# Weight sums of a second mixture by accumulating DMAs of GpSimd's queue, and four products of its layer one kept in one PSUM bank

## The chip, the cores and the metric

One core of a Trainium2 chip runs the whole program. The metric is the device time of one execution in microseconds. The engines are named as in the profile: PE is TensorE (PEld its weight load), ACT is ScalarE, DVE is VectorE, POOL is GpSimd, SP is SyncE. A queue that only issues DMAs carries a q (SPq, POOLq).

## The reference, cut to what matters

The program computes an attention with hashed buckets, a first mixture of experts (one expert per token) and a second mixture. The change touches the second mixture alone:

```
def _moe2_ref(x, w_gate, w1, w2):            # x (768, 512), w1 (8, 512, 1024), w2 (8, 1024, 512)
    ...                                      # P (768, 8): the gate, normalised 8 times by rows and columns
    for e in range(8):
        h = np.maximum(x @ w1[e], 0.0)       # layer one
        ye = h @ w2[e]                       # layer two
        out += P[:, e:e + 1] * ye
    return out
```

## The kernel before, in words

Before the second mixture come attention and the first mixture (to about 264 us of the span); both stay as they are.

Second mixture. Numbers are kept as pairs of halves (a high and a low part in float16), so that one product in full precision is three matmuls per 128 rows of the contraction. Expert 0 runs plainly (`plain`, then `gemm2(0)`), the experts 1 to 7 each run `gemm1(e)` and `gemm2(e)`.

`gemm1(e)` computes x times w1[e] with seven products in place of eight. x is cut in four blocks (two halves of the tokens by two halves of the 512 inputs), w1[e] in four quarters A(fh, dh) of 256 inputs (dh) by 512 outputs (fh). The products stand in the order of `PROD`, i = 0 to 6. Each needs one block, or a sum of blocks, of x (made once, `sum_x`), and one quarter, or a sum of quarters, of w1: i = 0, 1 and 6 take the quarters A(0,0), A(0,1) and A(1,1) as they are; i = 2 to 5 take sums of two to four quarters. A product is cut by four chunks j of 128 outputs. For one (i, j), six matmuls of 128x384 go into one PSUM bank; below that is a *group*, and an expert has 28 of them. Behind each group ACT or DVE takes the bank out:

- before, i = 0 is copied to `ta` by ACT (L1688); i = 1 accumulates on top of i = 0 in the same bank, ACT takes its relu (L1690) and the high part of it (L1653), DVE the low part (`low`, L1654);
- i = 2, 3, 4 each have a bank of their own, and DVE adds them to what it holds in SBUF (`add`, L1650); i = 5 and 6 share a bank, DVE adds twice;
- results go through `relu`: the high part by ACT (L1653), the low part by DVE (L1654).

Three matters set the order around this. The weights come by DMA into `raw` tiles (1 MB each, four per expert, an eight-tile ring, issued by SP, L313 and L315). `cut` turns a quarter or a sum into a slot of halves: `hi` by ACT (L1399), then `lo` by DVE (L1402). The sums of quarters are made by DVE just ahead of that (`combo`, L1589, four of 128x1024 per expert). ACT also sums the squares of each raw tile for a scale (`square_w`, L982, two per tile), which PE adds up over the partitions (`norm`, L990). All of these stand as tasks in one list; `work` takes one per group of `gemm1` and one or two per step of `gemm2`, so that most of an expert's cuts and sums run during `gemm2` of the expert before it. Each engine works its own instructions strictly in the order of the program.

`gemm2(e)` computes the second layer into six banks over four rounds r; in the last round DVE scales each bank and adds it to the result (L1774).

Of the kernel before, what the change touches and what calls it, by code (L numbers as in the profile page):

```python
# [8 lines left out]
F32 = mybir.dt.float32  # L9
# [12 lines left out]
P = 128  # L22
# [6 lines left out]
E = 8  # L29
# [193 lines left out]
def kernel(ctx: ExitStack, tc: tile.TileContext, consts, q, k, v, proj, wg, w1, w2, wg2, w12, w22, out, cap, dbg=None):  # L223
# [1154 lines left out]
    def base(e):  # L1378
        return NO0 + NO * (e - 1) if e else 0
# [12 lines left out]
    def cut(n, src=None):  # L1392
        e, i = place_of(n)
        sw = scl[:, 0 if i < 7 else 1, e:e + 1]

        def hi():
            if n not in slot:
                slot[n] = slot_tile(n)
            nc.scalar.activation(out=slot[n][:, 0], in_=src() if src else total[n], func=AF.Copy, scale=sw)  # L1399

        def lo():
            V.scalar_tensor_tensor(  # L1402
                out=slot[n][:, 1], in0=src() if src else total.pop(n), scalar=sw, in1=slot[n][:, 0],
                op0=ALU.mult, op1=ALU.subtract,
            )

        return [hi, lo]
# [81 lines left out]
    def sum_x(o):  # L1489

        for c in range(2):
            in0, in1 = {
                XT1: (ta[:, c], tb[:, c]), XT2: (ta[:, 2 + c], xf(XT1, c)), XT3: (xf(XT2, c), tb[:, c]),
                XT4: (tb[:, 2 + c], xf(XT2, c)),
            }[o]
            V.tensor_tensor(out=xf(o, c), in0=in0, in1=in1, op=ALU.subtract)

    held_x = []
    combine(0)
# [83 lines left out]
    def w1q(e, fh, dh):  # L1583
        return raw_t[4 * NV + 4 * e + fh][:, 2 * dh:2 * dh + 2, :]

    def combo(n, in0, in1, op):
        def go():
            total[n] = sums.tile([P, 2, 512], F32, tag="s", name="s")
            V.tensor_tensor(out=total[n], in0=in0(), in1=in1(), op=op)  # L1589

        return go

    def sums_of(e):
        a = lambda fh, dh: (lambda: w1q(e, fh, dh))
        n = base(e)
        of = lambda m: (lambda: total[n + m])
        return [
            combo(n + 3, a(1, 0), a(1, 1), ALU.add), combo(n + 2, of(3), a(0, 0), ALU.subtract),
            combo(n + 4, a(0, 1), of(2), ALU.subtract), combo(n + 5, a(0, 0), a(1, 0), ALU.subtract),
        ]  # L1600
# [11 lines left out]
    def alloc():  # L1612
        n = state["alloc"]
        if n >= base(E):
            return
        state["alloc"] += 1
        e, i = place_of(n)
        load = [lambda: load_next(nc.scalar if e == 0 else nc.sync)]
        if i > 6:
            r, h = divmod(i - 7, 2)  # L1620
            todo = sq(e + 1, 0, r) if i in (8, 9) else []
            todo = todo + cut(n, lambda: raw_t[4 * NV + 4 * e + 2 + r][:, 2 * h:2 * h + 2, :]) + load * h
        elif e == 0:
            todo = cut(n, lambda: w1q(e, i // 2, i % 2)) + load
            if i == 3:
                todo = todo + sq(e, 1, 0) + sq(e, 1, 1) + [none] * 2 + scale(e, 1)
        elif i < 2:
            todo = ([none] * 2 + scale(e, 0) if i == 0 else []) + cut(n, lambda: w1q(e, 0, i))
            todo = todo + (sums_of(e)[0:2] if i == 0 else sums_of(e)[2:3])
        elif i < 6:  # L1630
            todo = cut(n) + (sums_of(e)[3:4] + load if i == 3 else sq(e, 1, i - 4) if i > 3 else [])
        else:
            todo = cut(n, lambda: w1q(e, 1, 1)) + load + [none] * 2 + scale(e, 1)
        tasks.extend((n, f) for f in todo)
# [11 lines left out]
    blk = lambda b, j, fh, th: hT[:, b, 4 * fh + j, halves[th]]  # L1646
    lows = []

    def add(ps, out, in1):
        V.scalar_tensor_tensor(out=out, in0=ps, scalar=HSH, in1=in1, op0=ALU.mult, op1=ALU.add)  # L1650
# [13 lines left out]
    def gemm1(e):  # L1664
        held, kept = {}, []
        for i, o in enumerate(PROD):
            w = slot[base(e) + i]
            for j in range(4):
                again = i in (1, 6)
                if again:  # L1670
                    ps = held.pop(j)
                    free.append(kept.pop(0))
                elif i in (0, 5):
                    ps = held[j] = bank(kept)
                else:
                    ps = bank()
                n = 0
                ps = ps[:, 0:HW]
                for c in range(2):
                    for a, b in W3:  # L1680
                        nc.tensor.matmul(  # L1681
                            ps, lhsT=w[:, a, c, j * P:(j + 1) * P], rhs=xo[:, o, b, c, :],
                            start=(n == 0 and not again), stop=(n == 5), skip_group_check=again,
                        )
                        n += 1
                u, v, w12_ = ta[:, j], tb[:, j], tcc[:, j % 3]
# [166 lines left out]
```

## Time and profile before

| | us |
|---|---|
| median of 3 runs | 751.83 (750.5 to 755.17) |
| the profiled execution | 750.09 |
| its span | 748.3 |
| second mixture, as part of the span | about 264 to 748 |

The page gives each engine's busy time; the views of stretches and of instructions in order of time give the second mixture, whose seven experts repeat a pattern of some 58.6 us each.

### The profile page before, as it was taken

To read this page: it belongs to the slowest core of one execution; us is meant where nothing else is said; L and a number is where in the kernel's file an instruction comes from. 1 tells how busy PE (TensorE), PEld (TensorE's weight loads), DVE (VectorE), ACT (ScalarE), POOL (GpSimd) and SP (SyncE) were. 2 spreads that over 40 slices of the span, in tenths; PEclk is the share of its full clock that TensorE was granted. 3 is DMA by queue.
4 is the path that set the end of the run, shared out by engine and by line. 5 is a ranking of instruction groups with operands and counts; after the bars stand their busy time and mean duration, and the time that the engine had idled before them with its cause. 6 is when DMAs were issued, how large, how long until landed. Compare 5 with 4: busy or idle time off the path is not lost.

```text
span 748.3 us, 12168 instructions
## 1 busy us (share of the span) xinstructions
PE 725.5 (97%) x4700; PEld 465.2 (62%) x4700; DVE 568.3 (76%) x989; ACT 465.1 (62%) x757; POOL 114.8 (15%) x110
## 2 busy tenths in 40 slices
PE   6899998999999799999999999999999999999998
PEld 6798987877788556545545545545545545645654
DVE  5999998589999866887695785786785865866842
ACT  4698898388788678555653754664575375365420
POOL 5568883612100300000000000000000000000000
PEclk9999998999999999999999999999999999999999
DMA  9546559799998333422131131041033030000002
GB/s 228 128 124 170 157 153 361 276 380 378 385 378 305 88 113 113 168 73 98 63 108 56 38 131 58 3 164 59 1 115 112 1 113 1 1 1 0 1 1 85
DMA packets 61608, 97.02 MB, mean 130 GB/s; under 512 B 17603, under 2 KB 19059, under 8 KB 61546
## 3 DMA queue, kind: packets, MB, share of 16 engines
q1 hardware_dynamic: 53066, 82.21, 33.6%
q10 hardware_dynamic: 7520, 10.83, 4.2%
q0 software_dynamic: 960, 3.15, 1.3%
q8 instruction: 39, 0.64, 0.3%
q14 instruction: 23, 0.19, 0.1%
HBM read 79.99 MB, written 9.31 MB: 119 GB/s over the span
## 4 chain that ended last, share of the span: by engine, by line
PE 62%; DVE 2%; ACT 1%; issue 0%; DVEq 0%
PE b L1756 32%; PE b L1681 25%; PE b L1724 4%; DVE hl L1402 1%; DVE s L1589 1%; PE b L1519 1%; ACT junk L982 0%; DVE q L1253 0%; DVE x L1772 0%; PE b L1478 0%; PE b L990 0%; PE b L1466 0%; ACT hl L1399 0%; PE b L1566 0%; DVE x L1257 0%
## 5 line engine op out<-in xcount | busy, mean ns | idle before, releaser
L1756 PE MATMUL b<-hl,hT 128*128 128x512 f16 (+1 forms) x1176 | 252.0, 375 | 0.0
L1756 PEld LDWEIGHTS <-hT 128*128 128x128 f16 x1176 | 114.3, 98 | 129.1
L1681 PE MATMUL b<-xo,hl 128*128 128x384 f16 x1176 | 192.7, 326 | 0.0
L1681 PEld LDWEIGHTS <-hl 128*128 128x128 f16 x1176 | 114.7, 98 | 77.0 <-issue 0.8
L1402 DVE SCALAR_TENSOR_TENSOR hl<-raw,scl,hl 128x1024 f16<-128x1024 f32 x57 | 72.3, 1281 | 45.0 <-ACT hl L1399 45.0
L338 DVE TENSOR_TENSOR hl<-raw,hl 128x1024 fp32r<-128x1024 f32 x66 | 81.9, 1284 | 4.1 <-ACT hl L336 3.9
L1399 ACT ACTIVATE hl<-raw,scl 128x1024 f16<-128x1024 f32 x57 | 63.1, 1136 | 24.8 <-DVE scl L993 24.8
L336 ACT ACTIVATE hl<-raw 128x1024 fp32r<-128x1024 f32 x72 | 71.8, 1059 | 1.4 <-PE av L770 0.9
L982 ACT ACTIVATE junk<-raw 128x1024 bf16<-128x1024 f32 x64 | 67.1, 1048 | 1.0
L1774 DVE SCALAR_TENSOR_TENSOR x<-b,q,x 128x512 f32<-128x512 f32 (+1 forms) x43 | 31.5, 737 | 34.4 <-PE b L1756 34.0
L1181 PE MATMUL mm<-hl,dT 128*128 128x512 f32 x216 | 54.3, 398 | 1.6 <-DVE dT L1154 1.6
L1654 DVE SCALAR_TENSOR_TENSOR hT<-tz,hT 128x384 f16<-128x384 f32 x44 | 24.1, 555 | 37.6 <-ACT hT L1653 37.4
L761 POOL TENSOR_TENSOR plo<-pf,phi 128x768 f16<-128x768 f32 x30 | 49.3, 1660 | 21.4 <-ACT phi L757 18.7
L1653 ACT ACTIVATE hT<-tc 128x384 f16<-128x384 f32 x28 | 14.6, 523 | 60.2 <-DVE tc L1650 60.2
L1207 PE MATMUL y<-hl,hT 128*128 128x512 f32 x192 | 49.2, 400 | 1.1 <-DVE ysb L1225 1.0
L1399 ACT ACTIVATE hl<-s,scl 128x1024 f16<-128x1024 f32 x28 | 31.4, 1145 | 28.5 <-DVE s L1589 21.5
L750 ACT ACTIVATE pf<-mm 128x384 f32<-128x384 f32 x96 | 42.3, 492 | 10.2 <-PE mm L743 9.2
L696 DVE TENSOR_REDUCE mz<-mm 128x1 f32<-128x384 f32 x96 | 46.9, 547 | 0.9 <-PE mm L689 0.7
L1181 PEld LDWEIGHTS mm<-hl,dT 128*128 128x128 f32 x216 | 39.4, 188 | 10.6 <-DVE dT L1154 2.4
L743 PE MATMUL mm<-q,k 128*128 128x384 f32 x192 | 44.6, 354 | 0.4 <-DVE k L653 0.3
L757 ACT ACTIVATE phi<-pf 128x768 f16<-128x768 f32 x48 | 40.5, 850 | 1.6 <-PE av L770 0.3
L1207 PEld LDWEIGHTS y<-hl,hT 128*128 128x128 f32 x192 | 34.8, 188 | 9.1 <-DVE ysb L1225 1.8
(278 smaller groups left out, 1002.3 us busy)
## 6 DMA issues: line engine op xcount, KB each, us to landing
raw<-in_moe_w_dram SPq DMA_DIRECT2D x48, 1024.0 KB
raw<-in_moe_w_dram SPq DMA_DIRECT2D x48, 256.0 KB
raw<-in_moe_w_dram ACTq DMA_DIRECT2D x8, 1024.0 KB
xd<-zer SPq DMA_DIRECT2D x13, 256.0 KB
xe<-xd SPq DMA_DIRECT2D x7, 256.0 KB
yd<-ysb ACTq DMA_DIRECT2D x7, 256.0 KB
qkin<-in_q_dram SPq DMA_DIRECT2D x8, 192.0 KB
vin<-in_v_dram SPq DMA_DIRECT2D x4, 384.0 KB
```

Of the source, the lines that this page charges most:

```text
L336: nc.scalar.activation(out=t[:, 0], in_=raw[:, sl, :], func=AF.Copy)
L338: lo = lambda eng=eng, sl=sl, t=t: eng.tensor_tensor(out=t[:, 1], in0=raw[:, sl, :], in1=f32(t)[:, 0], op=ALU.subtract)
L696: V.tensor_reduce(out=mz[h][:, a, t:t + 1], in_=b.ps[:, 0:HW], axis=AX.X, op=ALU.max)
L743: nc.tensor.matmul(ps[:, 0:HW], lhsT=kk[h][:, tok(t)], rhs=qq[h][:, half(a)], start=(i == 0), stop=(i == 1))
L761: eng.tensor_tensor(out=lo[h, t], in0=pf[h, t], in1=hi[h, t], op=ALU.subtract)
L982: nc.scalar.activation(out=junk[:, 0:n], in_=src, func=AF.Square, accum_out=acc)
L1181: nc.tensor.matmul(ps, lhsT=dT[e][:, a, c * P:(c + 1) * P], rhs=w(b, c), start=(n == 0), stop=(n == 11))
L1207: nc.tensor.matmul(ps, lhsT=t[:, a, half, f * P:(f + 1) * P], rhs=w(b, f), start=(n == 0), stop=(n == 23))
L1399: nc.scalar.activation(out=slot[n][:, 0], in_=src() if src else total[n], func=AF.Copy, scale=sw)
L1402: V.scalar_tensor_tensor(out=slot[n][:, 1], in0=src() if src else total.pop(n), scalar=sw, in1=slot[n][:, 0], op0=ALU.mult, op1=ALU.subtract,)
L1681: nc.tensor.matmul(ps, lhsT=w[:, a, c, j * P:(j + 1) * P], rhs=xo[:, o, b, c, :], start=(n == 0 and not again), stop=(n == 5), skip_group_ ...
L1756: nc.tensor.matmul(ps, lhsT=hT[:, a, 2 * r + f, t * P:(t + 1) * P], rhs=w[:, b, f, cs], start=(r == 0 and n == 0), stop=(r == 3 and n == 5),)
```

## The change

1. **Sums of quarters.** `combo` and DVE's four additions per expert go. `combine_w` makes them out of DMAs: SP loads one quarter (512 KB) into a tile of `sums`, and GpSimd's queue adds the other quarters to it by DMAs with `accum_op=add`. The sum of i = 2 takes two such additions, i = 4 three, i = 5 one; the sum of i = 3 is made in place, by one addition of A(1,1) onto A(1,0) in the `raw` tile, after ACT has squared it. They are issued one expert ahead: those of i = 2, 4 and 5 right behind the cut that frees the tile of `sums`, that of i = 3 behind the squares. For expert 1 the first six stand at the start of the second mixture.
2. **Signs.** All sums are now additions, so the second half of the outputs is computed with the opposite sign; `sum_x` and the joins of `gemm1` turn it back.
3. **One bank for four products.** i = 0, 2, 3 and 4 now accumulate in one bank per j. ACT copies what stands in it after i = 0 (`ta`), i = 2 (`tb`) and i = 3 (`tz`), and takes the relu after i = 4. i = 1 has a bank of its own, which DVE joins to `ta` (`join`); i = 5 and 6 share a bank, joined to `tz` and `tb`. Per expert DVE has 12 joins where it had 20 additions; ACT has 16 copies out of PSUM where it had 8.
4. **Loads.** The load of the next expert's first raw tile moves from slot 3 to slot 1 of the task list.

```
-    def combo(n, in0, in1, op):
-            total[n] = sums.tile([P, 2, 512], F32, tag="s", name="s")
-            V.tensor_tensor(out=total[n], in0=in0(), in1=in1(), op=op)
...
+    def quarter(e, fh, dh):
+        return w12[e, dh * 256:dh * 256 + 256, fh * 512:fh * 512 + 512].rearrange("(c p) f -> p c f", p=P)
+
+    def combine_w(e, m):
+
         def go():
+            if m == 3:
+                t, parts = w1q(e, 1, 0), [(1, 1)]
+            else:
+                t = sums.tile([P, 2, 512], F32, tag="s", name="s")
+                parts = {2: [(0, 0), (1, 0), (1, 1)], 4: [(0, 0), (0, 1), (1, 0), (1, 1)], 5: [(0, 0), (1, 0)]}[m]
+                nc.sync.dma_start(out=t, in_=quarter(e, *parts.pop(0)))
+            for p in parts:
+                nc.gpsimd.dma_start(out=t, in_=quarter(e, *p), accum_op=ALU.add)
+            total[base(e) + m] = t
...
-            todo = sq(e + 1, 0, r) if i in (8, 9) else []
+            todo = sq(e + 1, 0, r) + (combine_w(e + 1, 3) if r else []) if i in (8, 9) else []
...
-            todo = todo + (sums_of(e)[0:2] if i == 0 else sums_of(e)[2:3])
+            todo = todo + (load if i == 1 else [])
         elif i < 6:
-            todo = cut(n) + (sums_of(e)[3:4] + load if i == 3 else sq(e, 1, i - 4) if i > 3 else [])
+            todo = cut(n) + (combine_w(e + 1, i) if i != 3 else []) + (sq(e, 1, i - 4) if i > 3 else [])
...
+    def copy(ps, out, func=AF.Copy):
+        nc.scalar.activation(out=out, in_=ps, func=func, scale=HSH)
+
+    def join(ps, t, sign):
+        V.scalar_tensor_tensor(
+            out=t, in0=ps, scalar=sign * HSH, in1=t, op0=ALU.mult, op1=ALU.add if sign > 0 else ALU.subtract
+        )
...
-                again = i in (1, 6)
...
+                key = (i > 4, j)
+                again = i in (2, 3, 4, 6)
+                if i in (0, 5):
+                    held[key] = bank(kept)
+                ps = bank() if i == 1 else held[key]
...
                 if i == 0:
-                    nc.scalar.activation(out=u, in_=ps, func=AF.Copy, scale=HSH)
+                    copy(ps, u)
                 elif i == 1:
-                    nc.scalar.activation(out=tz[:, j], in_=ps, func=AF.Relu, scale=HSH)
-                    relu(j, (0, 0), tz[:, j])
+                    join(ps, u, 1)
+                    relu(j, (0, 0), u)
                     low(0)
                 elif i == 2:
-                    add(ps, u, u)
+                    copy(ps, t)
                 elif i == 3:
-                    add(ps, v, u)
+                    copy(ps, v)
                 elif i == 4:
-                    add(ps, w12_, v)
-                    relu(j, (0, 1), w12_)
+                    copy(ps, r, AF.Relu)
+                    relu(j, (0, 1), r)
                 elif i == 5:
-                    add(ps, v, v)
+                    join(ps, v, -1)
                     relu(j, (1, 1), v)
                 else:
-                    add(ps, u, u)
-                    relu(j, (1, 0), u)
+                    join(ps, t, -1)
+                    relu(j, (1, 0), t)
...
+    for m in (2, 4, 5):
+        combine_w(1, m)[0]()
```

What the change makes of the order of three engines follows. First DVE in `gemm1(2)`, before: the low parts of i = 1 (`hT<-tz`, L1654), with the low half of slot 7 (L1402) in their midst, then the additions of i = 2 (`ta<-b`), i = 3 (`tb<-b`) and i = 4 (`tc<-b`).

```order
L1654 SCALAR_TENSOR_TENSOR hT_4395<-tz,hT_4395 128x384 x2
L1402 SCALAR_TENSOR_TENSOR hl<-raw,scl,hl 128x1024
L1654 SCALAR_TENSOR_TENSOR hT_4395<-tz,hT_4395 128x384 x2
L1650 SCALAR_TENSOR_TENSOR ta<-b,ta 128x384 x4
L1650 SCALAR_TENSOR_TENSOR tb<-b,ta 128x384 x4
L1650 SCALAR_TENSOR_TENSOR tc<-b,tb 128x384 x2
```

The same place of the changed kernel (its line 1660 is `join`, 1666 the low part): each j of i = 1 is a join, then the low part that waits for ACT's relu of that join.

```order
L1660 SCALAR_TENSOR_TENSOR ta<-b,ta 128x384
L1666 SCALAR_TENSOR_TENSOR hT_4395<-ta,hT_4395 128x384
L1660 SCALAR_TENSOR_TENSOR ta<-b,ta 128x384
L1666 SCALAR_TENSOR_TENSOR hT_4395<-ta,hT_4395 128x384
L1402 SCALAR_TENSOR_TENSOR hl<-raw,scl,hl 128x1024
L1660 SCALAR_TENSOR_TENSOR ta<-b,ta 128x384
L1666 SCALAR_TENSOR_TENSOR hT_4395<-ta,hT_4395 128x384
L1660 SCALAR_TENSOR_TENSOR ta<-b,ta 128x384
L1666 SCALAR_TENSOR_TENSOR hT_4395<-ta,hT_4395 128x384
L1666 SCALAR_TENSOR_TENSOR hT_4395<-tc,hT_4395 128x384 x3
```

DVE now has eight instructions for i = 1 in turn with ACT, and none for i = 2, 3 and 4 but the low parts; the low half of slot 7 still stands in their midst. ACT at this place, in the changed kernel (line 1657 is `copy`, 1665 the relu, 1399 the high half of a slot):

```order
L1657 ACTIVATE ta<-b 128x384 x4
L1665 ACTIVATE hT_4395<-ta 128x384
L1399 ACTIVATE hl<-raw,scl 128x1024
L1665 ACTIVATE hT_4395<-ta 128x384 x3
L1657 ACTIVATE tb<-b 128x384 x4
L1657 ACTIVATE tz<-b 128x384 x4
```

The copies of i = 2 (`tb<-b`) stand behind all four relus of i = 1, each of which waits for DVE's join. In the program the first matmul of each group of i = 3 waits for ACT: for the copy of that j of i = 2. Last, the end of GpSimd's queue, before:

```order
L1244 DMA x<-yd,idxg 128x512 x6
L1364 UNCONDITIONAL_BRANCH
L1364 ISA
L1364 UNCONDITIONAL_BRANCH
L1830 UNCONDITIONAL_BRANCH
```

And in the changed kernel, of which the last two rows stand five more times:

```order
L1244 DMA x<-yd,idxg 128x512 x6
L1364 UNCONDITIONAL_BRANCH
L1364 ISA
L1364 UNCONDITIONAL_BRANCH
L1604 DMA s<-in_moe_w_dram 128x2x512 x6
L1604 DMA raw<-in_moe_w_dram 128x2x512
L1604 DMA s<-in_moe_w_dram 128x2x512 x6
L1604 DMA raw<-in_moe_w_dram 128x2x512
```

GpSimd's queue had nothing to do in the second mixture; it has seven DMAs of 512 KB for each of the experts 1 to 7. Each addition waits for the DMA before it that wrote the same tile.

## Rows read from the trace of the kernel before

**Rows 1.** The page: its span, busy time of the engines

```profile
span 748.3 us, 12168 instructions
PE 725.5 (97%) x4700; PEld 465.2 (62%) x4700; DVE 568.3 (76%) x989; ACT 465.1 (62%) x757; POOL 114.8 (15%) x110
```

**Rows 2.** Stretches: length, busy us of each engine, granted clock, DMA share, GB/s

```profile
264.00:334.00 70.00, 70.00 (x411) 38.17 (x410) 53.08 (x135) 46.92 (x84) 0.00 (x0) 1.00 0.35 121
334.00:337.60 3.60, 2.90 (x23) 1.79 (x21) 3.60 (x6) 3.47 (x6) 0.00 (x0) 1.00 0.58 180
337.60:744.00 406.40, 406.40 (x2235) 214.85 (x2235) 279.31 (x437) 212.25 (x335) 0.00 (x0) 1.00 0.16 53
```

**Rows 3.** Timeline of PE: start, length (us), instruction, count, idle before it

```profile
337.52 0.16 PE L990 MATMUL b<-acc,ones 128*128 128x1 bf16 x1 [0.69 <-ACT junk L982]
...
393.20 27.46 PE L1681 MATMUL b<-xo,hl 128*128 128x384 f16 x168
...
627.52 27.46 PE L1681 MATMUL b<-xo,hl 128*128 128x384 f16 x168
```

**Rows 4.** Chain of waits, `gemm1` of expert 2: start, length

```profile
393.36 27.30 PE b L1681 x168
```

**Rows 5.** The page, groups by line: count, busy us, mean ns, idle before

```profile
L1774 DVE SCALAR_TENSOR_TENSOR x<-b,q,x 128x512 f32<-128x512 f32 (+1 forms) x43 | 31.5, 737 | 34.4 <-PE b L1756 34.0
```

**Rows 6.** Timeline of ACT in `gemm1(2)` (the 410.57 row: relu after a DVE addition)

```profile
398.27 0.49 ACT L1690 ACTIVATE tz<-b 128x384 f32<-128x384 f32 x1 [0.48 <-PE b L1681]
398.80 0.52 ACT L1653 ACTIVATE hT<-tz 128x384 f16<-128x384 f32 x1
399.23 1.13 ACT L1399 ACTIVATE hl<-raw,scl 128x1024 f16<-128x1024 f32 x1
400.26 0.47 ACT L1690 ACTIVATE tz<-b 128x384 f32<-128x384 f32 x1
...
410.57 0.52 ACT L1653 ACTIVATE hT<-tc 128x384 f16<-128x384 f32 x1 [7.41 <-DVE tc L1650]
```

**Rows 7.** Timeline of DVE in `gemm1(2)`

```profile
392.86 0.15 DVE L993 TENSOR_SCALAR scl<-scl 128x1 int32<-128x1 int32 x1
...
399.35 0.56 DVE L1654 SCALAR_TENSOR_TENSOR hT<-tz,hT 128x384 f16<-128x384 f32 x1 [5.20 <-ACT hT L1653]
...
409.98 0.56 DVE L1650 SCALAR_TENSOR_TENSOR tc<-b,tb 128x384 f32<-128x384 f32 x1 [0.42 <-PE b L1681]
...
411.43 0.55 DVE L1654 SCALAR_TENSOR_TENSOR hT<-tc,hT 128x384 f16<-128x384 f32 x1
411.93 0.56 DVE L1650 SCALAR_TENSOR_TENSOR tc<-b,tb 128x384 f32<-128x384 f32 x1
```

**Rows 8.** Timeline, a slot's two halves: ACT's `hi`, DVE's `lo` (322.48 and on)

```profile
321.30 2.19 ACT L1399 ACTIVATE hl<-raw,scl 128x1024 f16<-128x1024 f32 x2 [11.11 <-DVE scl L993]
...
322.48 1.28 DVE L1402 SCALAR_TENSOR_TENSOR hl<-raw,scl,hl 128x1024 f16<-128x1024 f32 x1 [1.22 <-ACT hl L1399]
323.68 1.22 DVE L1589 TENSOR_TENSOR s<-raw 128x1024 f32<-128x1024 f32 x1
...
328.41 1.28 DVE L1402 SCALAR_TENSOR_TENSOR hl<-s,scl,hl 128x1024 f16<-128x1024 f32 x1
```

**Rows 9.** Timeline of ACT, cuts and squares ahead of expert 2

```profile
368.53 0.19 ACT L982 ACTIVATION_READ_ACCUMULATOR junk<-raw 128x1 bf16 x1
...
372.96 2.19 ACT L1399 ACTIVATE hl<-raw,scl 128x1024 f16<-128x1024 f32 x2 [2.16 <-DVE scl L993]
377.85 3.48 ACT L1399 ACTIVATE hl<-s,scl 128x1024 f16<-128x1024 f32 x3 [2.71 <-DVE s L1589]
```

**Rows 10.** Line 1244, GpSimd's DMAs of 256 KB: issue ns min/median/max; landing

```profile
L1244 POOL DMA_INDIRECT x<-yd,idxg x6: 947/950/1964, 241.5 to 249.1; - x6
...
DMA to landing us min/median/max: 3.5/3.7/5.2
```

**Rows 11.** The page, DMA queues: packets, MB, share of 16 engines' span

```profile
q0 software_dynamic: 960, 3.15, 1.3%
```

More of the change, by code (lines that the diff above doesn't have):

```diff
@@ L1492, in sum_x @@
             in0, in1 = {
-                XT1: (ta[:, c], tb[:, c]), XT2: (ta[:, 2 + c], xf(XT1, c)), XT3: (xf(XT2, c), tb[:, c]),
-                XT4: (tb[:, 2 + c], xf(XT2, c)),
-            }[o]
-            V.tensor_tensor(out=xf(o, c), in0=in0, in1=in1, op=ALU.subtract)
+                XT1: (tb[:, c], ta[:, c]), XT2: (xf(XT1, c), ta[:, 2 + c]), XT3: (xf(XT2, c), tb[:, c]),
+                XT4: (xf(XT2, c), tb[:, 2 + c]),
+            }[o]
+            if o == XT1:
+                V.tensor_tensor(out=xf(o, c), in0=in0, in1=in1, op=ALU.subtract)
+            else:
+                V.scalar_tensor_tensor(
+                    out=xf(o, c), in0=in0, scalar=-1.0, in1=in1, op0=ALU.mult, op1=ALU.subtract
+                )
     held_x = []
@@ L1584, in w1q @@
         return raw_t[4 * NV + 4 * e + fh][:, 2 * dh:2 * dh + 2, :]
-    def combo(n, in0, in1, op):
+    def quarter(e, fh, dh):
+        return w12[e, dh * 256:dh * 256 + 256, fh * 512:fh * 512 + 512].rearrange("(c p) f -> p c f", p=P)
+    def combine_w(e, m):
         def go():
-            total[n] = sums.tile([P, 2, 512], F32, tag="s", name="s")
-            V.tensor_tensor(out=total[n], in0=in0(), in1=in1(), op=op)
[L1591 to L1600, printed above, removed]
+            if m == 3:
+                t, parts = w1q(e, 1, 0), [(1, 1)]
+            else:
+                t = sums.tile([P, 2, 512], F32, tag="s", name="s")
[4 more added lines that the diff above has]
+            total[base(e) + m] = t
+        return [go] if 0 < e < E else []
     def sq(e, k, half):
@@ L1647 @@
     lows = []
-    def add(ps, out, in1):
-        V.scalar_tensor_tensor(out=out, in0=ps, scalar=HSH, in1=in1, op0=ALU.mult, op1=ALU.add)
+    def copy(ps, out, func=AF.Copy):
+        nc.scalar.activation(out=out, in_=ps, func=func, scale=HSH)
+    def join(ps, t, sign):
+        V.scalar_tensor_tensor(
+            out=t, in0=ps, scalar=sign * HSH, in1=t, op0=ALU.mult, op1=ALU.add if sign > 0 else ALU.subtract
+        )
     def relu(j, at, src):
@@ L1668, in gemm1 @@
             for j in range(4):
-                again = i in (1, 6)
-                if again:
-                    ps = held.pop(j)
+                key = (i > 4, j)
[3 more added lines that the diff above has]
+                ps = bank() if i == 1 else held[key]
+                if i in (4, 6):
                     free.append(kept.pop(0))
[L1673 to L1676, printed above, removed]
                 n = 0
@@ L1682, in gemm1 @@
                             ps, lhsT=w[:, a, c, j * P:(j + 1) * P], rhs=xo[:, o, b, c, :],
-                            start=(n == 0 and not again), stop=(n == 5), skip_group_check=again,
+                            start=(n == 0 and not again), stop=(n == 5), skip_group_check=True,
                         )
                         n += 1
-                u, v, w12_ = ta[:, j], tb[:, j], tcc[:, j % 3]
+                u, v, t, r = ta[:, j], tz[:, j], tb[:, j], tcc[:, j % 3]
                 if i == 0:
-                    nc.scalar.activation(out=u, in_=ps, func=AF.Copy, scale=HSH)
+                    copy(ps, u)
                 elif i == 1:
-                    nc.scalar.activation(out=tz[:, j], in_=ps, func=AF.Relu, scale=HSH)
-                    relu(j, (0, 0), tz[:, j])
+                    join(ps, u, 1)
+                    relu(j, (0, 0), u)
                     low(0)
                 elif i == 2:
-                    add(ps, u, u)
+                    copy(ps, t)
                 elif i == 3:
-                    add(ps, v, u)
+                    copy(ps, v)
                 elif i == 4:
-                    add(ps, w12_, v)
-                    relu(j, (0, 1), w12_)
+                    copy(ps, r, AF.Relu)
+                    relu(j, (0, 1), r)
                 elif i == 5:
-                    add(ps, v, v)
+                    join(ps, v, -1)
                     relu(j, (1, 1), v)
                 else:
-                    add(ps, u, u)
-                    relu(j, (1, 0), u)
+                    join(ps, t, -1)
+                    relu(j, (1, 0), t)
                 if i > 3:
```

## Prediction

> **What bounds the kernel now.** I looked first at the stretches of the second mixture [rows 2]. The reader is to see that PE is busy for all of 264 to 334 us and for all of 337.6 to 744 us, at a granted clock of 1.00, with DVE at 69% and ACT at 52% of the last stretch. Then at PE in order of time [rows 3]: its one idle piece there is 0.69 us at 336.8, where `norm` waits for ACT's squares. The chain of waits [rows 4] is PE alone through an expert; its 28 groups last 27.30 us, 0.975 us each, so group k (counted from 0) starts 0.975k behind the first. So PE's work bounds this part, and the change alters neither the number nor the shape of its matmuls. What it takes off DVE was hidden; at most the 0.69 us can be won. The question is whether something makes PE wait that did not before.
>
> **DVE's additions, the signs, the loads.** Four additions of 1.22 us (the 323.68 row of [rows 8]) for seven experts are 34 us of DVE; eight fewer joins at 0.56 us [rows 7] for seven are 31 us more. Both lie under PE's matmuls: nothing on the path. With the sums gone, ACT's cuts no longer wait for them (2.71 us before the third cut in [rows 9], likewise in expert 1), so ACT's squares come before PE's `norm` and the 0.69 us go: −0.7. The signs change one kind of DVE instruction for another of the same size, under `plain`, where PE is without a gap: nothing. The load in slot 1 is only earlier.
>
> **One bank for four products.** This adds waits. A group of i = 2 may start when ACT has copied that j of i = 0: eight groups lie between start and start, so seven (6.8 us) are left; no wait. A group of i = 3 (k = 12 to 15) must wait for ACT's copy of that j of i = 2 (k = 8 to 11), with three groups, 2.9 us, between. ACT is in order, and ahead of those copies stand the four relus of i = 1, each waiting for DVE's join of that j; on DVE each join stands behind the low part of the j before, which waits for that relu. So the four j go hand over hand. The steps have rows: join to relu 0.59 us (DVE 409.98, ACT 410.57) [rows 6, 7]; relu to low part 0.55 (398.80, 399.35) [rows 6, 7]; low part to the next DVE addition 0.50 (411.43, 411.93) [rows 7]. That is 1.64 us for a j, where PE takes 0.975. The first join can start 0.19 behind the end of group 4: the copy of that same group started 5.07 us into the expert (398.27 less 393.20) [rows 3, 6].
>
> Experts 2, 4 and 6, in us from the expert's first matmul: join0 5.07, join1 6.71, low1 7.85; then the low half of slot 7, which the order puts here, at 8.35 for 1.20 (322.48 to 323.68 in [rows 8]); join2 9.55, join3 11.19, relu3 11.78; 0.43 on (relu to the next ACT instruction, 398.80 to 399.23) the first copy of i = 2 at 12.21, done 0.49 later at 12.70 [rows 6]. Group 12 was due at 12 × 0.975 = 11.70: **PE waits 1.0 us**. The next copies follow every half microsecond, so only one group waits.
>
> Experts 3, 5 and 7 have that low half behind the joins, and two scalars (0.15 us each [rows 7], 0.35 with their issue) in their midst: join2 8.70, relu2 9.29, join3 10.34. ACT's high half of slot 7 stands ahead of relu3, from 9.72 to 10.75 (1.03, 399.23 to 400.26 [rows 6]): relu3 10.93, copy done 11.85: **0.1 us**. Expert 1 has both halves of slot 7 ahead of the joins: `ta` is copied at 4.1, the high half starts at 4.5, the low half 1.18 behind (321.30, 322.48 [rows 8]), 5.7 to 6.9; join0 6.9, join3 11.8, relu3 12.4, copy done 13.3: **1.6 us**. Behind i = 3 the copies have 2.9 us again, and ACT's copy and relu of one j (0.96 us from 398.27 to 399.23 [rows 6]) keep pace in i = 4; i = 5 to 6 goes by DVE's joins, as it did. Sum: 3 × 1.0 + 3 × 0.1 + 1.6 = **4.9 us**.
>
> **The accumulating DMAs.** None is in the trace. The nearest rows are GpSimd's gathers of 256 KB: 0.95 to 1.96 us on GpSimd, 3.5 to 5.2 us from issue to landing [rows 10]. An addition moves 512 KB and must read what it adds to. From below it costs such a gather's least, 3.5 us. From above twice the slowest, 10.4 us. In between: that queue moved 3.15 MB in 1.3% of 748.3 us, 324 GB/s [rows 1, 11]; 256 KB are 0.8 us of the 3.7; 512 KB by three streams in place of two are 2.4 us; so T = 3.7 − 0.8 + 2.4 = 5.3 us, my estimate. The Trainium skill, page "DMA: Bandwidth & Descriptors", section "Anatomy of one DMA — SWDGE (gpsimd) path", has a fit of 2.0 us plus the bytes over 436 GB/s. By it 512 KB would take 3.2 us (an estimate; it names no accumulation), and a 256 KB gather 2.6 us, where the trace has 3.5 at the least; the measurement decides, and the sum would be the same by either.
>
> Where does T matter? Seven in a row are 37 us, an expert lasts 58.6 (393.20 to 627.52 us is four) [rows 3]. The tightest is the sum made in place: issued behind the squares (368.72), wanted by ACT as the fourth cut, at 372.96 plus three cuts of 1.1, some 376.3 [rows 9]: 7.6 us against 5.3. Were it later, ACT and DVE would wait, with more cuts, squares and the six bank additions of the last round queued behind it, and PE only when its third group needs the first y bank, at 393.20 + 1.95 = 395.15. Between stand the cut (1.18), two low halves (2.4) and one bank addition (0.75) [rows 5, 8]: the cut may start at 390.8, 14.5 us later than wanted. The plain loads are ahead of the additions by the same queue's measure (3.7 us). So I cost the DMAs at nothing; the cover is PE's matmuls, and it is gone where T is over 8.2 (below).
>
> **Sum.** 750.09 + 4.9 − 0.7 = 754.3 us against the profiled execution; the median of the three runs is 1.74 above that one, and I add half of it: **755.2 us**, a loss of about half a percent.
>
> **Rivals.**
>
> 1. *No wait at the bank.* If the hand-over between DVE and ACT is quicker than its rows, or DVE gets ahead, PE keeps its pace. For it: in three experts of seven the sum misses by only 0.1 us. Against: the other four miss by 1.0 or more, through a low half whose length is known. Time: 750.09 − 0.7 = 749.4, to 751.1 by the median.
> 2. *The additions are too slow, and the kernel is clearly slower.* GpSimd's queue works them one by one. Those for expert 2 can begin when expert 1's third cut has freed its tile (329.6 [rows 8]) and a load has come (3.7 us): 333.3. Seven must be there by 390.8: T up to 8.2 us is free. At T = 9: 333.3 + 63 = 396.3, 5.5 late, then 63 − 58.6 = 4.4 more for each of five experts: 27.5 us, 778. At the bound of 10.4: 15.3 + 5 × 14.2 = 86 us, 836. Against it: an addition into another tile need not wait for the one before, only for its own load, so two of the seven steps overlap but for some 1.2 us of issue, and then five steps bound the queue, free up to (58.6 − 2.5) / 5, about 11 us. For it: nothing here shows how fast a DMA adds in SBUF.
> 3. *A longer hand-over in all experts.* If each of its twelve steps costs 0.2 us more, PE waits 2.4 us more in each of seven experts: 17 us, some 771.
> 4. *Faster.* PE's one gap bounds the gain at 0.7 us. Only shorter matmuls could give more, and nothing alters them.
>
> **How the numbers follow.** The forecast 0.6; rival 1 0.2; rival 2 0.14; rival 3 0.05; rival 4 0.01. Rival 1 is within reach, so the range begins at 749.4; above it takes the forecast with double its wait (759), and rivals 2 and 3 only in their beginnings: T = 8.6 gives 333.3 + 60.2 = 393.5, 2.7 late, and 1.6 more for each of five, 10.7 in all: 765. The forecast's own range is 752 to 759. One per cent, about 7.5 us, is what a measurement of this kernel can tell from no change. The forecast and rival 1 lie within it; rivals 2 and 3 beyond. Faster 0.02, same 0.79, slower 0.19.
>
> **What the changed profile would show.** PE in order of time has a gap ahead of group 12 of `gemm1`, put down to ACT's copy line, about 1 us in experts 2, 4 and 6, 1.6 in expert 1, hardly any in 3, 5 and 7; the gap ahead of `norm` at 336.8 is gone; group length stays 0.975 us at a clock of 1.00. GpSimd's additions land some 5 us after issue and its queue idles part of each expert. The prediction is wrong if PE waits before a group whose weights come from a sum (a late DMA), if ACT's cut of a sum waits for a DMA by over 14 us, or if the gap ahead of group 12 is absent or several us long.

## The result, and the profile after

| | before | after |
|---|---|---|
| median (16 runs of each, timed together) | 751.65 us (749.34 to 755.17) | 756.49 us (753.49 to 759.23) |
| ratio, 95% interval | | 1.0056 [1.0039, 1.0073] |
| the profiled execution | 750.09 us | 753.77 us |
| its span | 748.3 us | 752.0 us |

The changed kernel is slower by about half a percent, 3.7 us between the two profiled executions. The forecast was 755.2 us, with a range of 749.4 to 765.

The page of the changed kernel, its span and the busy time of the engines, against [rows 1]:

```profile
span 752.0 us, 12235 instructions
PE 726.7 (97%) x4700; PEld 464.1 (62%) x4700; DVE 510.0 (68%) x905; ACT 488.7 (65%) x813; POOL 173.9 (23%) x159
q0 software_dynamic: 14288, 28.84, 22.1%
```

DVE has lost 58 us of work, ACT has 24 more, GpSimd's queue moves 28.84 MB where it moved 3.15 [rows 11]. PE has the same 4700 matmuls. The second mixture in the same stretches as [rows 2] (length, busy us of PE, PEld, DVE, ACT, POOL, granted clock, DMA share, GB/s):

```profile
264.00:334.00 70.00, 70.00 (x412) 38.27 (x410) 52.27 (x135) 50.10 (x89) 6.95 (x6) 1.00 0.56 130
334.00:337.60 3.60, 3.60 (x28) 2.21 (x26) 2.38 (x3) 2.40 (x4) 0.00 (x0) 1.00 1.01 215
337.60:744.00 406.40, 402.40 (x2209) 212.34 (x2208) 220.46 (x352) 233.81 (x387) 49.85 (x41) 1.00 0.56 134
```

The short stretch is full now, where PE had waited for `norm`; the long one, which was full, lacks 4.0 us. The granted clock is 1.00 throughout, so these are waits and not slower matmuls. The waits of PE in the second mixture (us in total, times, longest):

```profile
PE b L1692 <- ACT tb L1657: 4.0, 4, 1.4
```

That is the only entry: `gemm1`'s matmuls (line 1692, before 1681) for ACT's copy (1657). Where these four stand, by PE in order of time (start, length, count, idle before it):

```profile
333.87 3.09 PE L1692 MATMUL b<-xo,hl 128*128 128x384 f16 x18
...
347.21 3.09 PE L1692 MATMUL b<-xo,hl 128*128 128x384 f16 x18 [1.38 <-ACT tb L1657]
...
394.09 11.86 PE L1692 MATMUL b<-xo,hl 128*128 128x384 f16 x72
406.82 15.76 PE L1692 MATMUL b<-xo,hl 128*128 128x384 f16 x96 [0.87 <-ACT tb L1657]
422.42 2.75 PE L1767 MATMUL b<-hl,hT 128*128 128x512 f16 x12
...
525.02 15.76 PE L1692 MATMUL b<-xo,hl 128*128 128x384 f16 x96 [0.88 <-ACT tb L1657]
643.21 15.76 PE L1692 MATMUL b<-xo,hl 128*128 128x384 f16 x96 [0.87 <-ACT tb L1657]
```

The gap stands behind 72 matmuls, that is 12 groups of six: ahead of group 12, in the experts 1, 2, 4 and 6 and in no other. What a gap costs is read better from the length of a whole `gemm1` than from the idle time in its row: expert 2 lasts 422.42 − 394.09 = 28.33 us, against 27.30 before [rows 4], so the gap of 0.87 costs 1.03. The same difference of starts gives 28.34 and 28.33 for experts 4 and 6, 27.40 for 3, 5 and 7 as before, and 28.94 for expert 1 (a `gemm1` of the odd experts has `norm`'s four small matmuls in its midst, 27.40 without a wait): 1.54 too much there. In sum 1.54 + 3 × 1.03 = 4.63 us lost. Expert 1 lasted 28.23 before, so the wait for `norm` had cost 0.83, and that is won. The balance is +3.80; the mixture started 0.18 later in this execution, and from DVE's last instruction to the end of the span, while the output lands, it took 0.3 us less: 3.7, the difference of the spans.

The chain that ended last shows the wait from inside. It is PE alone in [rows 4]; in expert 2 it now leaves PE behind group 4, counted from 0 (start, length, what):

```profile
394.23 4.91 PE b L1692 x30
...
399.24 0.57 DVE ta L1660
...
399.83 0.53 ACT hT L1665
...
400.39 0.56 DVE hT L1666
400.94 0.48 DVE ta L1660
...
402.56 1.20 DVE hl L1402
403.75 0.48 DVE ta L1660
...
405.37 0.48 DVE ta L1660
...
405.87 0.52 ACT hT L1665
406.39 0.39 ACT tb L1657
...
406.82 15.76 PE b L1692 x96
```

Four times join (L1660), relu (L1665), low part (L1666), hand over hand between DVE and ACT, with the low half of slot 7 (L1402, 1.20 us) after the second; then the first copy of i = 2, and PE may go on. The rows left out are pieces of 0.02 to 0.05 us between these, and the relus and low parts of the second and the third chunk, as long as those of the first. From join to join it is 1.62 us where nothing else lies between (405.37 − 403.75), against 0.975 for a group of PE.

GpSimd's accumulating DMAs (issue ns min/median/max; what the queue waited for; landing in us), with GpSimd in order of time for one expert:

```profile
L1604 POOL DMA_DIRECT2D s<-in_moe_w_dram x42: 1203/1209/1737, 255.8 to 647.8; - x42
L1604 POOL DMA_DIRECT2D raw<-in_moe_w_dram x7: 1203/1209/1222, 307.4 to 664.7; - x7
...
DMA to landing us min/median/max: 5.9/7.4/13.9
```

```profile
501.25 1.22 POOL L1604 DMA_DIRECT2D s<-in_moe_w_dram  x1 [12.68 <-DMA s<-in_moe_w_dram]
507.92 2.44 POOL L1604 DMA_DIRECT2D s<-in_moe_w_dram  x2 [5.44 <-DMA s<-in_moe_w_dram]
520.55 1.20 POOL L1604 DMA_DIRECT2D s<-in_moe_w_dram  x1 [10.19 <-DMA s<-in_moe_w_dram]
529.90 2.45 POOL L1604 DMA_DIRECT2D s<-in_moe_w_dram  x2 [8.15 <-DMA s<-in_moe_w_dram]
546.53 1.21 POOL L1604 DMA_DIRECT2D raw<-in_moe_w_dram  x1 [14.18 <-ACT junk L982]
560.98 1.20 POOL L1604 DMA_DIRECT2D s<-in_moe_w_dram  x1 [13.25 <-DMA s<-in_moe_w_dram]
```

Seven per expert. An addition alone keeps the next one waiting 6.67 us (501.25 to 507.92) or 9.35 (520.55 to 529.90); after two issued together into different tiles it is 12.63 (507.92 to 520.55). These times are not fixed. For expert 1, at the start of the mixture, such a pair kept the next one waiting 9.06 us:

```profile
262.42 2.47 POOL L1604 DMA_DIRECT2D s<-in_moe_w_dram  x2 [5.28 <-DMA s<-in_moe_w_dram]
271.48 1.21 POOL L1604 DMA_DIRECT2D s<-in_moe_w_dram  x1 [6.60 <-DMA s<-in_moe_w_dram]
```

That is less than two alone (two times 6.67). The first pair of the other experts took 12.63 to 14.93 us. All DMAs together, these two among them, moved 143 GB/s in that stretch, and 220 to 325 GB/s in those of the slower pairs. Lone additions took 6.41 to 8.36 us at 140 to 243 GB/s, and 9.35 and 9.62 at 340 and 311. So the slow ones stand where other loads move much at the same time; that these are what slows them was not tested. The sum made in place is issued at 546.53, when ACT has squared the tile (L982), and the next expert's first addition at 560.98, when SP's load has come. Nothing waits here for the second pair; in the run with nine additions below the next one does, and it took 9.1 to 9.7 us for the experts from 2 on. With that, or with as much as the first pair at the most, and 6.3 us for the sum made in place (its median landing), the work of an expert is 6.67 + 12.63 + 9.35 + 9.1 to 12.63 + 6.3, some 44 to 48 us of 59.7. So the queue idles in each expert, but by 12 to 16 us and not by the 22 that 37 us of work would have left. ACT waits nowhere for the sum made in place.

### The profile page after: what moved, and what is told of

It is laid out like the page before. It is cut to its first block, busy times and chain, and to the rows that moved or that the text cites. A ratio compares the mean times of both kernels' runs of the same rounds, so it can differ in the third digit from the quotient of the medians.

```text
span 752.0 us, 12235 instructions
## 1 busy us (share of the span) xinstructions
PE 726.7 (97%) x4700; PEld 464.1 (62%) x4700; DVE 510.0 (68%) x905; ACT 488.7 (65%) x813; POOL 173.9 (23%) x159
## 3 DMA queue, kind: packets, MB, share of 16 engines
q0 software_dynamic: 14288, 28.84, 22.1%
## 4 chain that ended last, share of the span: by engine, by line
PE 60%; DVE 3%; ACT 2%; issue 0%; DVEq 0%
PE b L1767 33%; PE b L1692 22%; PE b L1735 4%; ACT hT L1665 1%; DVE ta L1660 1%; DVE hT L1666 1%; DVE hl L1402 1%; PE b L1524 1%; DVE q L1253 0%; ACT tb L1657 0%; PE b L1478 0%; PE b L1466 0%; PE b L990 0%; PE b L1571 0%; ACT hl L1399 0%
## 5 line engine op out<-in xcount | busy, mean ns | idle before, releaser
L1402 DVE SCALAR_TENSOR_TENSOR hl<-raw,scl,hl 128x1024 f16<-128x1024 f32 x64 | 80.6, 1281 | 46.3 <-ACT hl L1399 46.3
L1604 POOL DMA_DIRECT2D s<-in_moe_w_dram x42 | 51.3, 1385 | 253.4 <-DMA s<-in_moe_w_dram 247.9
L1399 ACT ACTIVATE hl<-raw,scl 128x1024 f16<-128x1024 f32 x64 | 71.1, 1136 | 24.1 <-DVE scl L993 24.1
L1785 DVE SCALAR_TENSOR_TENSOR x<-b,q,x 128x512 f32<-128x512 f32 (+1 forms) x43 | 31.5, 737 | 57.1 <-PE b L1767 57.1
L982 ACT ACTIVATE junk<-raw 128x1024 bf16<-128x1024 f32 x64 | 67.1, 1048 | 1.0
L1657 ACT ACTIVATE ta<-b 128x384 f32<-128x384 f32 x28 | 13.7, 490 | 52.3 <-PE b L1692 52.1
L1666 DVE SCALAR_TENSOR_TENSOR hT<-tc,hT 128x384 f16<-128x384 f32 x28 | 15.6, 556 | 44.4 <-ACT hT L1665 44.4
```

The lines of the kernel that those rows point to most:

```text
L982: nc.scalar.activation(out=junk[:, 0:n], in_=src, func=AF.Square, accum_out=acc)
L1402: V.scalar_tensor_tensor(out=slot[n][:, 1], in0=src() if src else total.pop(n), scalar=sw, in1=slot[n][:, 0], op0=ALU.mult, op1=ALU.subtract,)
L1604: nc.gpsimd.dma_start(out=t, in_=quarter(e, *p), accum_op=ALU.add)
```

## The experiments

Two theories. **Hand-over:** all of the loss is the wait ahead of group 12, which comes from where the relus of i = 1 stand in ACT's order. Rivals: the loss belongs to one bank for four products as such (a bank cannot be read and written in such a rhythm), or to the 26 MB of accumulating DMAs. In all ratios the kernel before, run beside the experiment, is 1.

### The relus of i = 1 behind the copies of i = 2

```
                 elif i == 1:
                     join(ps, u, 1)
-                    relu(j, (0, 0), u)
-                    low(0)
                 elif i == 2:
                     copy(ps, t)
+                    relu(j, (0, 0), u)
+                    low(0)
```

> ScalarE's relu and VectorE's low part of product 1 are written behind the copy of product 2 of the same chunk; all else as in the changed kernel. Theory (the hand-over between VectorE and ScalarE holds up the copies on which group 12 waits): the four gaps ahead of group 12, 4.0 us in the changed kernel's trace (1.38, 0.87, 0.88, 0.87), are all gone, TensorE has no gap from 264 to 744 us, and the time is the kernel before's less 0.7 for the gap ahead of the norm plus 0.2 that the changed kernel starts the experts later: some 751.2 us against 751.65, ratio 0.998 to 1.001. Rival 1 (four products in one bank cost time by themselves, whatever stands ahead of the copies): gaps of about 1 us stay in four experts, ratio 1.0056. Rival 2 (the accumulating DMAs cost the time, through the memory or the queues): no change from the changed kernel, 1.0056.

Measured: 750.96 us (12 runs), ratio 0.9976 [0.9960, 0.9991]; the kernel before had 752.67 there. PE in expert 1 and 2, no gap and the old length:

```profile
337.75 24.54 PE L1692 MATMUL b<-xo,hl 128*128 128x384 f16 x150
...
393.40 27.46 PE L1692 MATMUL b<-xo,hl 128*128 128x384 f16 x168
420.70 4.48 PE L1767 MATMUL b<-hl,hT 128*128 128x512 f16 x20
```

Each relu of i = 1 now stands behind the copy of i = 2 of the same chunk. Same bank, same copies, same joins, same DMAs; only the order differs, and 420.70 − 393.40 is 27.30 again. So it is not the bank as such, and not the DMAs. This version is faster than the changed kernel and, by its interval, a little faster than the kernel before: from the first matmul of the gate (L1519 before, L1524 after) to the end of the span it has 482.6 us (748.2 − 265.59) against 483.7 (748.3 − 264.57).

### No weight work between the joins

```
+                if i == 1:
+                    continue
                 if i < 4:
-                    work(2 if e == 1 else 1, base(e) + 7)
+                    work(1, base(e) + 7)
```

> No task of the list is taken while product 1 runs, so both halves of slot 7 stand behind the joins; the hand-over itself stays as it is. Theory: without the low half's 1.2 us the first copy of product 2 is done at 11.5 us where group 12 is due at 11.7, in all seven experts: gaps of 0.1 us at the most, in the sum under 0.5, time some 751.3 us, ratio 0.998 to 1.001. If the hand-over alone is already too slow (rival: the low half does not matter): gaps of some 0.5 to 0.9 us in all seven experts, 3.5 to 6 us, ratio 1.004 to 1.008. If the accumulating DMAs cost the time: 1.0056 as before.

Measured: 751.69 us (12 runs), ratio 0.9991 [0.9975, 1.0007]. PE has no listed gap; its busy time in the long stretch is 406.03 of 406.40 us, and expert 2 lasts 421.72 − 394.14 = 27.58, so 0.28 too much in place of 1.03 (expected: 0.1 at the most). Experts 4 and 6 have 27.58 too; 1, 3, 5 and 7 have 27.40, as without a wait. Expert 1 takes one task per group here where it took two:

```profile
394.14 27.74 PE L1692 MATMUL b<-xo,hl 128*128 128x384 f16 x168
421.72 3.62 PE L1767 MATMUL b<-hl,hT 128*128 128x512 f16 x16
```

The hand-over alone, four joins at 1.62 us, nearly fits into the time that PE gives it; the weight work in its midst is what breaks it.

### The low half of slot 7 twice

```
+            if i == 7 and e:
+                halves_of[1] = lambda lo=halves_of[1]: (lo(), lo())
```

> VectorE makes the low half of slot 7 twice in experts 1 to 7 (the second time the same values). Theory: 1.2 us more in the chain of experts 1, 2, 4 and 6, where this half stands ahead of a join, and nothing in 3, 5 and 7, where it stands behind the last: gaps 2.6, 2.1, 2.1, 2.1, 8.8 us in all, the time 4.8 us over the changed kernel's: some 761.3 us, ratio 1.012 to 1.014. Rivals (one bank in itself, or the accumulating DMAs): VectorE has time to spare (54% busy), so no change: 756.5, 1.0056.

Measured: 762.42 us (6 runs), ratio 1.0127 [1.0106, 1.0149].

```profile
PE b L1695 <- ACT tb L1660: 9.3, 4, 2.7
```

```profile
350.06 17.44 PE L1695 MATMUL b<-xo,hl 128*128 128x384 f16 x96 [2.70 <-ACT tb L1660]
```

The gaps are 2.70, 2.19, 2.20 and 2.19 us (1.38, 0.87, 0.88 and 0.87 in the changed kernel): each has grown by 1.3, a little more than the 1.20 us put in, and experts 3, 5 and 7 still have none. An instruction of DVE in that place goes into PE's time about one to one. The profiled execution lost a little more: behind the gap of 2.70 us in expert 1 the 96 matmuls last 17.44 us in place of 15.76, with the granted clock at 0.50 from 352 to 354 us, the lower of the two levels (1.2 and 2.4 GHz), and back at 1.00 from 354. From the gate's first matmul to the end it has 494.2 us (760.5 − 266.27), 7.0 more than the changed kernel's 487.3: the four gaps 5.3, the clock 1.7. A gap alone does not decide this: behind the 2.86 us in the run with the bank alone, below, the clock stayed at 1.00.

### The sums by DMA alone, banks as before

```
-                key = (i > 4, j)
-                again = i in (2, 3, 4, 6)
-                if i in (0, 5):
-                    held[key] = bank(kept)
-                ps = bank() if i == 1 else held[key]
...
+                again = i in (1, 6)
+                if again:
+                    ps = held.pop(j)
...
-                    copy(ps, t)
+                    add(ps, u, u)
```

> The sums by accumulating DMAs and the signs stay; the seven products use the banks as in the kernel before (product 1 on top of 0 by ScalarE, products 2, 3 and 4 each in a bank of its own, added by VectorE). Theory: no gap ahead of group 12 and none ahead of the norm, time the kernel before's less 0.7 plus 0.2: some 751.2 us, ratio 0.998 to 1.001. Rival (the accumulating DMAs cost the time): 756.5 us, 1.0056. If the hand-over is only part of it: in between.

Measured: 751.79 us (12 runs), ratio 0.9978 [0.9961, 0.9995]; no wait of PE from 264 to 744 us. From the gate's first matmul to the end it has 482.6 us, 1.1 less than the kernel before: 0.83 is the wait ahead of `norm`, 0.3 the stretch behind DVE's last instruction, as in the changed kernel. The accumulating DMAs cost PE nothing, and the bit that they free of DVE is worth that one wait.

### The bank alone, the sums by DVE

```
+    def combo(n, in0, in1, op):
...
+            total[n] = sums.tile([P, 2, 512], F32, tag="s", name="s")
+            V.tensor_tensor(out=total[n], in0=in0(), in1=in1(), op=op)
...
-            todo = sq(e + 1, 0, r) + (combine_w(e + 1, 3) if r else []) if i in (8, 9) else []
+            todo = sq(e + 1, 0, r) if i in (8, 9) else []
...
-    for m in (2, 4, 5):
-        combine_w(1, m)[0]()
```

> The four products in one bank and the joins as in the change, but the sums of quarters made by DVE again (all as sums with a plus sign, in the order of the tasks of the kernel before), no accumulating DMA. Hand-over theory: PE waits ahead of group 12 of gemm1 for the copy of i = 2 as in the changed kernel, 1.4 us in expert 1 and 0.9 in experts 2, 4 and 6, none in 3, 5 and 7, 4.0 in all, or a few tenths more where a sum on DVE falls between two joins; the 0.69 us ahead of norm come back, since ACT's cuts wait for DVE's sums again. So 4.7 us of gaps, 4 to 6 us over the kernel before, ratio 1.005 to 1.008. Rival (the accumulating DMAs are needed for the loss, by what they move in SBUF or on the queues): no gap ahead of group 12, ratio 0.999 to 1.001.

Measured: 760.3 us (6 runs), ratio 1.0107 [1.0090, 1.0125]: slower than expected.

```profile
340.35 0.16 PE L990 MATMUL b<-acc,ones 128*128 128x1 bf16 x1 [0.69 <-ACT junk L982]
352.18 15.76 PE L1690 MATMUL b<-xo,hl 128*128 128x384 f16 x96 [2.86 <-ACT tb L1655]
411.79 15.76 PE L1690 MATMUL b<-xo,hl 128*128 128x384 f16 x96 [0.88 <-ACT tb L1655]
```

The edit also puts the load of raw tiles back in slot 3. The gaps of experts 2, 4 and 6 (0.88 us each; the rows of 4 and 6 are not shown) and the wait for `norm` are those of the changed kernel and of the kernel before, to 0.01 us: the bank loses without any accumulating DMA. Expert 1 has 2.86 in place of 1.38. There ACT's cuts have waited for DVE's sums, 2.71 us at 329.02 and 2.14 at 336.93, so that the first copy of `ta` comes 3.7 us into the expert (1.2 in the changed kernel) and the high half of slot 7 behind it. Its low half, which stands ahead of the first join on DVE, starts 8.1 us into the expert (5.8 in the changed kernel), and the first join at 9.3 (7.0):

```profile
344.59 1.28 DVE L1402 SCALAR_TENSOR_TENSOR hl<-raw,scl,hl 128x1024 f16<-128x1024 f32 x1 [1.22 <-ACT hl L1399]
345.79 0.55 DVE L1658 SCALAR_TENSOR_TENSOR ta<-b,ta 128x384 f32<-128x384 f32 x1
```

So the two halves of the change are not independent: the sums by DMA save PE 0.83 us alone, the wait for `norm`, but 2.31 us where the one bank is in (`gemm1` of expert 1 lasts 31.25 here, `norm`'s wait included, and 28.94 in the changed kernel). From the gate to the end this kernel has 489.9 us, 6.2 more than the kernel before; the ratio says 6.8 to 9.4. The rest, at least 0.6 us, I cannot place.

### No accumulating DMAs at all

```
-            for p in parts:
-                nc.gpsimd.dma_start(out=t, in_=quarter(e, *p), accum_op=ALU.add)
```

> The changed kernel without its accumulating DMAs: each sum of quarters is only its first quarter, so a part of the computation is left out. Hand-over theory: the gaps ahead of group 12 stay as they are, 1.4, 0.9, 0.9 and 0.9 us, 4.0 in all, and the time stays within 1 us of the changed kernel's, ratio 1.004 to 1.007 against the kernel before. Rival (the 24 MB that the additions move cost time of their own): the time falls towards the kernel before, ratio 0.998 to 1.002. The loads that fill the tiles of sums stay, so GpSimd's gathers still land later (some 5.9 us at the median).

Measured: 756.81 us (6 runs), ratio 1.0052 [1.0032, 1.0073], as the changed kernel. The gaps stand where they stood:

```profile
PE b L1690 <- ACT tb L1655: 4.0, 4, 1.4
```

With 26 MB less on GpSimd's queue not a tenth of a microsecond of them has gone. The DMA theory falls here. Rival 2 of the prediction, additions too slow, had fallen with the changed profile, in which PE waits for no sum.

### Nine additions per expert

```
-            for p in parts:
+            for p in parts * (2 if m in (3, 5) else 1):
```

> The changed kernel with the additions of i = 3 and of i = 5 issued twice, nine per expert in place of seven, so two sums are not those of the reference. The prediction held up to 8.2 us for each of seven additions to be free, 57 us of queue per expert. By the trace of the changed kernel nine take 47 + 2 x 6.7, some 60 us, as long as an expert. Theory (the queue's time per expert is the bound, with some 14 us in hand before PE waits): the gaps ahead of group 12 stay, PE waits for no sum or by less than 2 us per expert, ratio 1.005 to 1.02. Rival (the cover is smaller, since the sum made in place is wanted soon behind the squares): PE waits by the 7 to 13 us that the two additions take, in each of experts 2 to 7, 40 to 80 us in all, ratio 1.05 to 1.11.

Measured: 756.63 us (5 runs), ratio 1.0047 [1.0029, 1.0066], no slower than the changed kernel. The waits of ACT in the second mixture have a new entry, and PE one new gap:

```profile
ACT hl L1399 <- DMA raw<-in_moe_w_dram: 34.7, 6, 9.8
```

```profile
387.26 1.15 ACT L1399 ACTIVATE hl<-raw,scl 128x1024 f16<-128x1024 f32 x1 [9.83 <-DMA raw<-in_moe_w_dram]
```

```profile
394.99 0.16 PE L990 MATMUL b<-acc,ones 128*128 128x1 bf16 x1 [0.43 <-ACT junk L982]
```

ACT's cut of the sum made in place now waits in six experts, by 9.83 us in expert 2 and by less than 6 in the others, and PE loses 0.43 us once, in expert 2. Both rows are of that expert: the cut may come some 9.4 us late there before PE waits, not the 14.5 that the prediction worked out. And PE waits at another place than it named, at `norm`, for ACT's squares (L982), which stand behind that cut in ACT's order.

### Fourteen additions per expert

```
-            for p in parts:
+            for p in parts + parts:
```

> The changed kernel with each accumulating DMA issued twice, 14 per expert in place of 7, so the sums are not those of the reference. In the changed kernel the seven keep GpSimd's queue for some 47 of the 59 us of an expert (from the first issue at 501.25 us to the landing of the sum made in place at some 548 to 552). Fourteen take some 94 us, 35 us more than an expert lasts: with the cover gone PE waits for the cut of a sum, in each of experts 2 to 7 but for what the first can draw on, 5 to 6 times 35 us, 175 to 210 us in all, so some 930 to 965 us. Rival (additions into different tiles overlap, so that the queue has twice the room that it needs): PE waits nowhere for a sum, and the time stays under 765 us.

Measured: 916.88 us (2 runs), ratio 1.2179 [1.2150, 1.2208]. The waits of ACT, and PE in order of time:

```profile
ACT hl L1399 <- DMA raw<-in_moe_w_dram: 213.7, 7, 36.2
```

```profile
596.49 1.15 ACT L1399 ACTIVATE hl<-raw,scl 128x1024 f16<-128x1024 f32 x1 [36.25 <-DMA raw<-in_moe_w_dram]
```

```profile
432.58 0.16 PE L990 MATMUL b<-acc,ones 128*128 128x1 bf16 x1 [21.64 <-ACT junk L982]
...
518.75 5.84 PE L1692 MATMUL b<-xo,hl 128*128 128x384 f16 x24 [18.40 <-DVE x L1785]
...
599.77 0.16 PE L990 MATMUL b<-acc,ones 128*128 128x1 bf16 x1 [22.45 <-ACT junk L982]
600.95 0.16 PE L990 MATMUL b<-acc,ones 128*128 128x1 bf16 x1 [1.02 <-ACT junk L982]
```

With the cover gone (the time by which a sum may be late before PE waits) the queue sets the pace, and the place that gives way is the one that the prediction named as the tightest, the sum made in place. PE then waits at two places. In experts 1, 2, 4 and 6 it waits for the squares behind that cut on ACT: in expert 4 ACT waits 36.25 us for the sum, and PE 22.45 us ahead of the first of `norm`'s four matmuls and 1.02, 1.92 and 1.02 ahead of the others, 26.4 in all. That is 9.8 less; in expert 2 it is 9.9 less, in expert 1 only 5.0 (18.68 against 13.69). In experts 3, 5 and 7 PE waits at its third group for DVE's bank additions (L1785), the place that the prediction had worked out: 18.40 us in expert 3, where ACT waits 29.22, so 10.8 less. Two experts last 599.77 − 432.58 = 167.2 us, one 83.6, so an addition in a full queue takes 6.0 us. I had expected 94 us for fourteen and a time from 930 us on; in a row they are quicker than with the idle time of the changed kernel counted in. The granted clock was 0.84 from 400 to 600 us here, a mean of the chip's two levels (2.4 and 1.2 GHz), with PE idle for up to 22 us at a time; since the queue sets the pace, no loss of its own is read from that.

## Why the prediction was right, point by point

- **PE bounds the second mixture, and the work taken off DVE is worth nothing.** Right. DVE lost 58 us, and the only thing won is the wait ahead of `norm`: 0.69 us forecast by its row, 0.83 measured by the length of `gemm1`.
- **The hand-over.** Right in place, cause and size. Forecast for experts 2, 4 and 6, from the first matmul: joins at 5.07, 6.71, 9.55 and 11.19 us, the copy at 12.21. The chain above, less 394.09: 5.15, 6.85, 9.66, 11.28 and 12.30, each up to 0.14 later. Most of that is the chain's way of giving the end of what lies before as the start: by DVE's own rows the second and the third join start at 400.86 and 403.67 (6.77 and 9.58), by ACT's own the copy at 406.30 (12.21). Loss 1.0 us forecast, 1.03 measured; expert 1 1.6 and 1.54; experts 3, 5 and 7 0.1 and none. Sum 4.9 forecast, 4.63 measured.
- **What was on the edge.** Experts 3, 5 and 7 were forecast to miss by 0.1 us and miss by nothing. Two small terms of the working went the other way there: DVE's two scalars hold up the third join by 0.26 us (461.91 to 462.17) and not by 0.35, and `norm`'s four matmuls in PE's order ahead of group 12, 0.10 us, were left out. The run without weight work between the joins shows the hand-over alone at 0.28 in experts 2, 4 and 6. The forecast was good because steps of half a microsecond had rows for the same shapes [rows 6 to 8]; it would have been a guess with a mean over lines.
- **The additions cost nothing.** Right in the sum, by three runs (without them, with them alone, with nine). The size was too small: T was estimated at 5.3 us, and an addition takes 6.0 in a full queue and 6.41 to 9.62 alone; it lands 5.9 to 13.9 us after issue, the longest beyond my upper bound of 10.4, which did not count that two can be under way, with SP's loads beside them. What was too quick in the working: bytes by the mean rate of the gathers, as if an addition only moved a third stream. I had 37 us of queue for an expert; it is some 44 to 48. Of the Trainium skill's fit (page "DMA: Bandwidth & Descriptors", section "Anatomy of one DMA — SWDGE (gpsimd) path"), which makes 3.2 us of 512 KB as an estimate, this case's trace shows no accumulating DMA that quick: the quickest lands in 5.9 us.
- **Where the additions would bite.** Right in the transfer, wrong in the cover, by a path that was left out. The sum made in place gives way first. But the prediction let PE wait only at the first y bank of its third group, and had a cover of 14.5 us. In experts 2, 4 and 6 PE has to pass `norm` before that, whose squares stand behind the same cut on ACT, and the cover is 9.4 to 9.9 us; at the y bank, in expert 3, it is 10.8. In expert 1 it is 5.0, but there the sum is issued at 307.40, 17 us before ACT's cut of it in the changed kernel (324.61). By the same sum the bound in T falls from 8.2 to some 7.5 us for seven in a row (an estimate from the 9.4), 52 us of queue in place of 57. The total did not hang on it, since ACT waits nowhere for that sum in the changed kernel; that is a margin that was large enough, not a working that was right. Nine additions, 54 us at 6.0 each, cost 0.43 us once; fourteen, 84 us, were not free. It was not narrowed further.
- **The loads at the start of the mixture.** Not in the prediction: SP now loads the first tiles of sums while GpSimd's gathers run, and these land 2.2 us later at the median [rows 10]:

```profile
L1244 POOL DMA_INDIRECT x<-yd,idxg x6: 946/949/1959, 241.7 to 249.3; - x6
...
DMA to landing us min/median/max: 4.5/5.9/7.3
```

  It cost nothing that can be seen: from the last gather's issue to the gate's first matmul it is 264.75 − 249.3 = 15.4 us, and 264.57 − 249.1 = 15.5 before.
- **The median.** I added half of the 1.74 us between the first median and the profiled execution. The changed kernel's median is 2.7 over its profiled execution. In the profiled executions such differences lie ahead of the mixture: the gate's first matmul starts between 264.57 and 271.59 us in the profiled executions here, in code that is the same in all, while the stages behind it repeat to some tenths where PE does not wait. Differences of a few microseconds are therefore read from that point on.

## What to carry to other kernels

When products share a bank, the copy that frees it for the next must not stand behind work that waits for another engine: list what is ahead of it on its own in-order queue, add up the hand-overs, and compare with the groups that the matmul engine has in hand. Here writing each of four relus behind the copy of its own chunk turned a loss of 0.56% into a gain of 0.24% [0.09, 0.40], with nothing else changed. And work taken off an engine that does not bound a stage is worth what waits for that engine there, in this kernel one wait of 0.83 us out of 58 us saved.

## What the runs showed of the hardware that was not expected

An accumulating DMA of 512 KB into SBUF took 5.9 us at the least in the changed kernel and 6.0 us for each in a full queue; GpSimd spends 1.21 us on the issue. Two into different tiles, issued together, took 9.06 us until the next could start where all DMAs moved 143 GB/s, and 12.63 to 14.93 where they moved 220 to 325; a lone one took 6.41 to 8.36 at 140 to 243 GB/s, 9.35 and 9.62 at 340 and 311. Why, no run isolates. A wait of PE costs 0.16 us more than the idle time in its row (0.87 listed, 1.03 by the length of `gemm1`; 1.38 and 1.54 in expert 1). The rows show where the 0.16 comes from: without a gap a row of PE starts 0.16 us before the listed end of the row ahead of it (393.20 + 27.46 = 420.66 for expert 2 in the kernel before, and its next row starts 27.30 behind 393.20), so a gap first uses up that overlap. Starts, not idle times, give the cost.
